# Attention and gated MLP on one core: v's copies loaded by two queues, and the order of all operations read from a table

## Chip, cores and metric

The kernel runs on one core of one Trainium2 chip. The metric is the device time of one execution in microseconds. The core has five engines that work side by side, each through its own list of instructions in a fixed order: TensorE (PE) multiplies matrices, VectorE (DVE), ScalarE (ACT) and GpSimd (POOL) work element by element, and SyncE (SP) starts transfers. Engines wait for each other through semaphores, and a wait at the head of an engine's list holds up all that stands behind it.

## What is computed

Attention with rotary embedding for 8 batches of 8 heads (576 positions, head width 64), and behind it a gated MLP whose gate mixes positions. Cut to what matters:

```python
q_rot, k_rot = (rotate(q), rotate(k))
scores = scale * np.matmul(q_rot, k_rot.transpose(0, 1, 3, 2))
scores = scores - np.max(scores, axis=-1, keepdims=True)
attn = np.exp(scores)
attn = attn / (np.sum(attn, axis=-1, keepdims=True) + 1e-09)
x = np.matmul(attn, v)                      # 8 heads side by side: (8, 576, 512)
...
h = np.maximum(x @ w_in, 0.0)               # 1024 wide
u, v = (h[..., :512], h[..., 512:])
v_n = (v - mu) / np.sqrt(var + 1e-06)       # over the 512 columns
v_s = np.einsum('ts,bsd->btd', w_spatial, v_n) + b_spatial[None, :, None]
return (u * v_s) @ w_out
```

## The kernel before

The work comes in 32 **units** (one batch, two heads) and 8 **MLPs** (one batch each, ready when its four units are done). Units and MLPs overlap: while the units of batch b run, PE fills the gaps between their score tiles with the matmuls of an earlier batch's MLP. The last MLP has nothing left to run beside it.

A unit from number 4 on goes through these steps:

- `prepare` loads q and k (tiles `st`), turns them on POOL, splits them into a rounded part and a rest, and SP copies the halves into the stacked tiles `stk` (ten copies a unit, `stk<-st` and `stk<-lk`), which PE reads.
- `scores` makes nine **score tiles** (128 rows by 576 columns) on PE, L782. A tile lies in one of two PSUM slots (`sc`, two banks each). For each tile DVE takes the maximum (L825), ACT the exponential (L828), which ends the slot's use, and DVE turns the result round in blocks of 32 (L830). PE's next tile but one needs the same slot again.
- `attention` multiplies the nine turned tiles with v, in two halves of 144 matmuls (L741), which use 32 rows of the array each. So v has to lie in the tile `vr` four times, once for each quarter of the partitions. `load_values` loads these four copies (320 KB each) with four transfers on SP. There is one such tile (`vrep`): the load of the next unit waits until the second half of this unit's product is through.
- ACT and DVE copy the product out of PSUM (L758, L759), `normalise` divides by the sums, and the result `x` waits for its MLP.

Units 0 to 3 are done in another way ("plain"): their weights are transposed on PE (L664, L667), copied out by ACT or DVE into one of six places in the tile `turns`, and multiplied there (L710); v is loaded once for them.

An MLP is four groups of matmuls: `pa` (L901, the normalised half), `pb` (L924, the other half), `pc` (L942, the mixing of positions, whose result multiplies u in `gate`) and `pd` (L957, the output). Each step of them is a piece of 2 or 3 matmuls of 288 or 512 columns, into one of four PSUM banks (`pm`), which the products with v use as well.

**What sets the order.** The functions above don't issue instructions. They hand operations to `Program.op`, with an engine, a duration, a due time (`key`, from the constants `K_...`) and the buffers read, written and newly needed. `Program.run` then plays the program through in a model of time: whenever an engine is free it takes, of the operations that are ready, the one with the lowest due time that finds a free slot for its buffers, and issues it. Operations that may run on two engines (`either`, `pair_op`) go to the one that is free first.

## Time and profile before

| | us |
|---|---|
| three runs | 833.79, 834.03, 838.24 |
| median of the runs | 834.03 |
| span of the profiled execution, first to last instruction | 831.4 |
| PE busy in it | 801.3 (96%) |
| PEld (weights loaded for PE) busy | 721.1 (87%) |
| DVE / ACT / POOL busy | 596.6 / 525.3 / 525.5 |

The span leaves out what lies around the first and the last instruction; the median of the runs is 2.6 us above it. PE's end of an instruction is modelled, and consecutive matmuls overlap: a matmul is shown with some 0.3 us, and the next may start 0.13 us after it. So a short stop of PE doesn't show as idle time, and a shown stop is a little longer than what stands there. The granted clock of PE is 0.97 of full speed in the first 50 us and 1.00 after that, the higher of its two levels.

### The profile page before, as it was taken

Reading aid. Unit: us, or ns where it says so; the run is one execution under the profiler, and the core shown is the slowest. Engines: PE = TensorE matmul, PEld = TensorE weight load, DVE = VectorE, ACT = ScalarE, POOL = GpSimd, SP = SyncE. Lnnn points to the kernel's source line nnn. Section 1 sums busy time; section 2 is a strip of 40 time slices with the busy share of each in tenths; the row PEclk is TensorE's granted clock in tenths of the full one; section 3 lists DMA queues with packets and bytes.
Section 4 is the critical chain, followed back from the end, with each engine's and each line's share of the span. In section 5 each row is a group of like instructions: output and inputs, shape, how many; then the busy total and the mean of one; then the engine's idle time right before and its main releaser. Section 6 shows DMA issues by size and latency. Waiting matters only on the chain.

```text
span 831.4 us, 30188 instructions
## 1 busy us (share of the span) xinstructions
PE 801.3 (96%) x12560; PEld 721.1 (87%) x12560; DVE 596.6 (72%) x1179; ACT 525.3 (63%) x1372; POOL 525.5 (63%) x440
## 2 busy tenths in 40 slices
PE   5999988999999999999999999999999999999998
PEld 3565678898899989998889989899899998999898
DVE  6879988886887669867686768776697766875220
ACT  4787877664865568656675648656586565844442
POOL 5998685786675667676566756767486675533221
PEclk9999999999999999999999999999999999999999
DMA  8755574779876777878847786777857778363001
GB/s 326 288 169 166 122 201 122 180 181 222 195 187 167 198 181 181 205 190 226 202 126 193 183 229 171 196 174 193 213 130 205 194 202 207 93 157 86 35 2 58
DMA packets 63867, 144.56 MB, mean 174 GB/s; under 512 B 10993, under 2 KB 12785, under 8 KB 63730
## 3 DMA queue, kind: packets, MB, share of 16 engines
q1 hardware_dynamic: 63730, 142.63, 66.3%
q8 instruction: 99, 1.62, 0.9%
q14 instruction: 38, 0.31, 0.1%
HBM read 93.55 MB, written 9.58 MB: 124 GB/s over the span
## 4 chain that ended last, share of the span: by engine, by line
PE 74%; DVE 7%; ACT 7%; DMA 5%; issue 3%; POOL 2%; SPq 1%; DVEq 0%; ACTq 0%; POOLq 0%
PE psum L741 15%; PE psum L942 14%; PE psum L782 13%; PE psum L957 10%; PE psum L901 9%; PE psum L924 7%; ACT et L828 4%; DMA vr<-in_v_dram 3%; DVE nmx L825 3%; PE psum L802 3%; PE psum L664 2%; PE psum L710 2%; DVE et L830 1%; SPq L416 1%; DVE sm L979 1%
## 5 line engine op out<-in xcount | busy, mean ns | idle before, releaser
L828 ACT ACTIVATE et<-psum,nmx 128x576 f32<-128x576 f32 x288 | 212.7, 740 | 111.1 <-DVE nmx L825 109.3
L825 DVE TENSOR_REDUCE nmx<-psum 128x1 f32<-128x576 f32 x288 | 210.9, 744 | 74.4 <-PE psum L782 64.7
L830 DVE STREAM_TRANSPOSE et<-et 128x576 f32<-128x576 f32 x252 | 192.7, 770 | 42.8 <-ACT et L828 40.7
L541 POOL TENSOR_TENSOR st<-st,tabs 128x576 f32<-128x576 f32 x112 | 163.0, 1468 | 64.1 <-DMA st<-in_qk_dram 49.5
L741 PE MATMUL psum<-et,vr 32*64 32x144 f32 x8064 | 142.7, 285 | 4.1 <-ACT vv L975 1.4
L741 PEld LDWEIGHTS psum<-et,vr 32*64 32x64 f32 x8064 | 126.8, 130 | 17.0 <-issue 11.1
L942 PE MATMUL psum<-wsp,vn 128*128 128x288 f32 x768 | 125.0, 296 | 1.2 <-issue 1.2
L924 PE MATMUL psum<-x,wi 128*128 128x288 f32 x768 | 118.9, 296 | 0.0
L957 PE MATMUL psum<-g,wo 128*128 128x288 f32 x768 | 117.4, 296 | 0.2
L901 PE MATMUL psum<-wi,x 128*128 128x512 f32 x448 | 117.6, 397 | 0.0
L942 PEld LDWEIGHTS psum<-wsp,vn 128*128 128x128 f32 x768 | 109.4, 188 | 2.6 <-issue 2.6
L924 PEld LDWEIGHTS psum<-x,wi 128*128 128x128 f32 x768 | 108.0, 188 | 3.8 <-issue 1.6
L957 PEld LDWEIGHTS psum<-g,wo 128*128 128x128 f32 x768 | 106.5, 188 | 2.5 <-issue 2.4
L782 PE MATMUL psum<-stk 128*128 128x288 f32 x448 | 99.4, 303 | 8.7 <-ACT et L828 8.3
L782 PE MATMUL psum<-stk,stk 128*128 128x288 f32 x448 | 95.7, 295 | 0.1
L901 PEld LDWEIGHTS psum<-wi,x 128*128 128x128 f32 x448 | 79.6, 188 | 16.4 <-issue 2.6
L422 POOL TENSOR_TENSOR g<-u,g 128x288 fp32r<-128x288 f32 x64 | 52.0, 816 | 63.7 <-ACT g L419 63.6
L782 PEld LDWEIGHTS psum<-stk 128*128 128x128 f32 x448 | 72.8, 188 | 19.8 <-ACT et L828 13.2
L545 POOL TENSOR_TENSOR st<-st 128x576 f32<-128x576 f32 x56 | 82.6, 1476 | 2.0
L422 POOL TENSOR_TENSOR vn<-vv,vn 128x512 fp32r<-128x512 f32 x32 | 41.3, 1293 | 61.8 <-ACT vn L419 61.8
L782 PEld LDWEIGHTS psum<-stk,stk 128*128 128x128 f32 x448 | 71.6, 188 | 0.2 <-issue 0.2
L422 POOL TENSOR_TENSOR x<-x,x 128x576 fp32r<-128x576 f32 x64 | 55.6, 890 | 17.2 <-ACT x L419 17.1
(134 smaller groups left out, 1012.3 us busy)
## 6 DMA issues: line engine op xcount, KB each, us to landing
vr<-in_v_dram SPq DMA_DIRECT2D x116, 320.0 KB
st<-in_qk_dram SPq DMA_DIRECT2D x62, 576.0 KB
stk<-lk SPq DMA_DIRECT2D x168, 144.0 KB
stk<-st SPq DMA_DIRECT2D x112, 128.0 KB
out_dram<-ob SPq DMA_DIRECT2D x31, 288.0 KB
ws<-in_w_spT_dram SPq DMA_DIRECT2D x2, 576.0 KB
st<-in_qk_dram SPq DMA_DIRECT2D x2, 288.0 KB
tabs<-in_tab_dram SPq DMA_DIRECT2D x2, 288.0 KB
```

The costliest lines, as they stand in the source:

```text
L422: eng.tensor_tensor(out=lo, in0=src, in1=hi.bitcast(F32), op=ALU.subtract)
L541: f = lambda e: e.tensor_tensor(out=st[j][:, cols], in0=st[j][:, cols], in1=tabs[:, cols], op=ALU.mult)
L545: f = lambda e: e.tensor_tensor(out=st[j][:, :S], in0=st[j][:, :S], in1=st[j][:, S:2 * S], op=ALU.add)
L741: nc.tensor.matmul(bank(g)[64 * h:64 * h + 64, EACH // 9 * (1 - h):EACH // 9 * (1 - h) + EACH], lhsT=vr[rows, b % 4, b // 4, h, :], rhs=e[ ...
L782: nc.tensor.matmul(pt[:, c * 512:c * 512 + HALF], lhsT=lhsT, rhs=rhs[:, c * HALF:(c + 1) * HALF], start=(n == 0), stop=(n == len(parts) - 1))
L825: op(DVE, 680, key + K_MAX, lambda: nc.vector.tensor_reduce(out=nmx.tile, in_=tops(), op=ALU.max, axis=AX.XY, negate=True), r=[pt], w=[nmx ...
L828: op(ACT, 750, key + K_EXP, lambda: nc.scalar.activation(weights(), tops(turn), AF.Exp, bias=nmx.tile, scale=1.0, accum_out=sm[:, to:to + ...
L830: op(DVE, 705, key + K_TURN, lambda: nc.vector.transpose(out=blocks(et, at), in_=blocks(et, at)), w=[(et, at)])
L901: nc.tensor.matmul(pm.tile, lhsT=lhsT, rhs=win[1, d][:, j, :], start=(d == 0 and n == 0), stop=(d == 3 and n == len(todo) - 1))
L924: nc.tensor.matmul(pm[:, :HALF], lhsT=win[0, d][:, i, f * P:(f + 1) * P], rhs=x[d][:, at:at + HALF], start=(d == 0 and n == 0), stop=(d == ...
L942: nc.tensor.matmul(pm[:, :HALF], lhsT=lhsT, rhs=rhs, start=(t == 0 and n == 0), stop=(t == 4 and n == 1))
L957: nc.tensor.matmul(pm[:, :HALF], lhsT=wout[d,][:, i, m * P:(m + 1) * P], rhs=gs[d][:, at:at + HALF], start=(d == 0 and n == 0), stop=(d == ...
```

## The change

In `load_values`, two of the four copies of v (partitions 0 to 63) are still started by SP, the other two (64 to 127) by ACT, with an operation of its own in ACT's list; the product with v then depends on both. `Program.run` no longer decides anything: it issues the operations in the order of a table, `ORDER`, a list of operation numbers; a letter behind a number says on which of its engines an operation that has a choice runs (a: ACT, v: DVE, g: POOL). A second table, `HOME`, gives the slot of each new buffer. The planner's model and most of its constants are gone. A few durations handed to `op` are others and a `mode` is given to it; nothing reads these any more. What each operation computes is as before.

```diff
+ORDER = """
+4 2 60 3 6 8 9 5 10 1 7 11 65 137 138 139 66 67 68 69 71 72 133 74 70 0 76 73 75 81 140v 141 309 77 79 214 12 82 13 78 215 54 22 49 134 84 80 14 83 85
...
+HOME = (
...
     def run(self, make):
-        free = {p: list(range(n)) for p, n in SLOTS.items()}
-        ready = {e: [] for e in LATENCY}
...
+
+        slots = iter(HOME)
+        for word in ORDER.split():
+            o = self.ops[int(word.rstrip("avg"))]
+            assert not o.waits, "an operation comes before one that it waits for"
             for b in o.new:
...
+                b.pool, b.slot = b.pools[0], int(next(slots))
+                b.tile = make(b)
+            o.eng = {"a": ACT, "v": DVE, "g": POOL}.get(word[-1], next(iter(o.costs)))
+            o.f(o.eng)
+            for a in o.after:
+                a.waits -= 1
+        assert next(slots, None) is None
...
-        def fetch():
+        def fetch(start, groups):
             rows = v[b, hp].rearrange("(q j) k h d -> j q (k h d)", q=4)
-            for g in range(4):
-                load(vr[32 * g:32 * g + 32].rearrange("j q k h d -> j q (k h d)"), rows)
-
-        op(DMA, dma_ns(1280, 4, 470, 5.23), key - K_LOAD + 1, fetch, w=[vr], new=[vr])
+            for g in groups:
+                start(out=vr[32 * g:32 * g + 32].rearrange("j q k h d -> j q (k h d)"), in_=rows)
+
+        o = op(DMA, dma_ns(640, 2, 470, 5.23), key - K_LOAD + 1, lambda: fetch(nc.sync.dma_start, (0, 1)), w=[(vr, 0), (vr, 2)], new=[vr])
+        op(ACT, dma_ns(640, 2, 470, 5.23), key - K_LOAD + 1, lambda: fetch(nc.scalar.dma_start, (2, 3)), w=[(vr, 1)], r=[(vr, 2)]).soft = o
...
-        need = [vr, *[(et, n) for n in range(9)]]
+        need = [(vr, 0), (vr, 1), *[(et, n) for n in range(9)]]
```

All five engines' lists change from one end to the other, mostly in small ways: units and MLPs follow each other as before, and neighbours change places. Lines of the file move as well (L782 becomes L786, L828 L831, L901 L904, L957 L960, L416 L420); the two starts of v are L507 now. Three places:

PE, the last score tiles of unit 24 (L782, four matmuls each over two rows: `stk_470` is the stack of the second head, `stk_471` the rests), with output pieces of MLP 4 (L957) between them. Before:

```order
L782 MATMUL psum<-stk_470 128x288 x2
L782 MATMUL psum<-stk_471,stk_470 128x288 x2
L957 MATMUL psum<-g_1_8485,wo_1099 128x288 x3
L782 MATMUL psum<-stk_470 128x288 x2
L782 MATMUL psum<-stk_471,stk_470 128x288 x2
L957 MATMUL psum<-g_2_8642,wo_2277 128x288 x3
L957 MATMUL psum<-g_3_8702,wo_2123 128x288 x3
L782 MATMUL psum<-stk_470 128x288 x2
L782 MATMUL psum<-stk_471,stk_470 128x288 x2
```

The first and the last of these three tiles use the same slot, and 3 + 4 + 6 = 13 matmuls lie between them. Now (the second head's stack is `stk_483`):

```order
L786 MATMUL psum<-stk_483 128x288 x2
L786 MATMUL psum<-stk_484,stk_483 128x288 x2
L960 MATMUL psum<-g_1_8479,wo_1087 128x288 x3
L960 MATMUL psum<-g_3_8729,wo_2120 128x288 x3
L960 MATMUL psum<-g_2_8652,wo_2224 128x288 x6
L786 MATMUL psum<-stk_483 128x288 x2
L786 MATMUL psum<-stk_484,stk_483 128x288 x2
L960 MATMUL psum<-g_3_8729,wo_2120 128x288 x3
L786 MATMUL psum<-stk_483 128x288 x2
L786 MATMUL psum<-stk_484,stk_483 128x288 x2
```

Again the first and the last of the three share a slot; 12 + 4 + 3 = 19 matmuls lie between them.

ACT, unit 16, around the start of its v (L828, then L831: exponentials of the unit's score tiles, named in `nmx` by head and tile; L960, then L963: outputs of MLP 2 out of PSUM). Before:

```order
L828 ACTIVATE et_5558,sums_67<-psum,nmx_0_2_5802 128x18x32
L960 ACTIVATE ob_2_5821<-psum 128x288 x2
L828 ACTIVATE et_5558,sums_67<-psum,nmx_0_3_5831 128x18x32
L828 ACTIVATE et_5558,sums_67<-psum,nmx_1_0_5849 128x18x32
L960 ACTIVATE ob_3_5868<-psum 128x288
L419 ACTIVATE x_5877<-x_15_5770 128x576
L828 ACTIVATE et_5558,sums_67<-psum,nmx_1_1_5880 128x18x32
```

Now:

```order
L831 ACTIVATE et_5548,sums_67<-psum,nmx_0_2_5791 128x18x32
L831 ACTIVATE et_5548,sums_67<-psum,nmx_0_3_5809 128x18x32
L507 DMA vr_5818<-in_v_dram 32x4x640 x2
L831 ACTIVATE et_5548,sums_67<-psum,nmx_1_0_5831 128x18x32
L423 ACTIVATE x_5856<-x_15_5762 128x576
L831 ACTIVATE et_5548,sums_67<-psum,nmx_1_1_5847 128x18x32
```

Two starts of transfers stand between the exponentials of tiles 0_3 and 1_0, and the outputs have moved away from there.

SP, its first transfers: q (`st_0`), k (`st_1`) and the tables of sines and cosines (`tabs`) of unit 0, each in two parts. Before:

```order
L416 DMA st_1_84<-in_qk_dram 128x2x288
L416 DMA tabs<-in_tab_dram 128x2x288
L416 DMA st_0_92<-in_qk_dram 128x2x192
L416 DMA st_1_84<-in_qk_dram 128x2x288
L416 DMA tabs<-in_tab_dram 128x2x288
L416 DMA st_0_92<-in_qk_dram 128x2x384
```

Now:

```order
L420 DMA st_0_79<-in_qk_dram 128x2x192
L420 DMA st_1_81<-in_qk_dram 128x2x288
L420 DMA tabs<-in_tab_dram 128x2x288 x2
L420 DMA st_1_81<-in_qk_dram 128x2x288
L420 DMA st_0_79<-in_qk_dram 128x2x384
```

The first part of q comes first, and the first part of the tables third.

## Rows read from the trace of the kernel before

**Rows 1.** The page's first part: busy time, share of the span and instructions by engine.

```profile
PE 801.3 (96%) x12560; PEld 721.1 (87%) x12560; DVE 596.6 (72%) x1179; ACT 525.3 (63%) x1372; POOL 525.5 (63%) x440
```

**Rows 2.** Busy time by stretch: us, each engine's busy us, clock, DMA share, GB/s.

```profile
0.00:50.00 50.00, 38.75 (x250) 22.96 (x252) 38.21 (x65) 31.57 (x75) 39.51 (x44) 0.97 0.76 276
50.00:100.00 50.00, 47.58 (x361) 30.89 (x357) 44.20 (x73) 43.18 (x112) 42.62 (x33) 1.00 0.54 151
```

**Rows 3.** Who PE waited for: us in total, times, the longest.

```profile
PE psum L782 <- ACT et L828: 8.6, 11, 1.6
PE psum L802 <- DVE st L614: 7.8, 1, 7.8
PE psum L664 <- DVE turns L675: 1.9, 2, 1.7
PE psum L741 <- ACT vv L975: 1.4, 1, 1.4
PE psum L741 <- DVE nmx L825: 1.3, 1, 1.3
```

**Rows 4.** The chain that ended last, a stretch of the last MLP: start, us, what.

```profile
816.54 11.66 PE psum L957 x87
```

**Rows 5.** The page's groups: busy us, mean ns of one, idle before.

```profile
L957 PE MATMUL psum<-g,wo 128*128 128x288 f32 x768 | 117.4, 296 | 0.2
```

**Rows 6.** PE in order of time, unit 24's last tiles: start, us, instruction, [idle before].

```profile
583.58 0.42 PE L782 MATMUL psum<-stk 128*128 128x288 f32 x2
...
584.49 0.42 PE L782 MATMUL psum<-stk 128*128 128x288 f32 x2
...
587.34 0.53 PE L782 MATMUL psum<-stk 128*128 128x288 f32 x2 [1.36 <-ACT et L828]
```

**Rows 7.** PE in order of time, stops at units 4, 16 (two) and 20.

```profile
96.21 0.53 PE L782 MATMUL psum<-stk 128*128 128x288 f32 x2 [1.25 <-ACT et L828]
...
391.29 0.53 PE L782 MATMUL psum<-stk 128*128 128x288 f32 x2 [0.59 <-ACT et L828]
...
392.31 0.40 PE L782 MATMUL psum<-lk,qt 128*128 128x288 f32 x1 [0.23 <-ACT et L828]
...
489.09 0.54 PE L782 MATMUL psum<-stk 128*128 128x288 f32 x2 [0.59 <-ACT et L828]
```

**Rows 8.** Weight loads of the plain units that waited for nothing shown.

```profile
PEld psum L710 <- issue: 5.1, 27, 0.4
```

**Rows 9.** DVE in order of time, the program's start.

```profile
4.97 0.76 DVE L608 TENSOR_TENSOR st<-st,tabs 128x576 f32<-128x576 f32 x1 [4.97 <-DMA tabs<-in_tab_dram]
5.76 0.46 DVE L609 TENSOR_TENSOR st<-st 128x288 f32<-128x288 f32 x1
6.78 0.56 DVE L613 SCALAR_TENSOR_TENSOR st<-st,tabs 128x384 f32<-128x384 f32 x1 [0.56 <-DMA st<-in_qk_dram]
7.37 0.36 DVE L614 TENSOR_TENSOR st<-st 128x192 f32<-128x192 f32 x1
8.38 0.76 DVE L608 TENSOR_TENSOR st<-st,tabs 128x576 f32<-128x576 f32 x1 [0.65 <-DMA tabs<-in_tab_dram]
```

**Rows 10.** The instructions on v's tile: ns of one, least, median, most; and idle causes.

```profile
L416 SPq DMA_DIRECT2D vr<-in_v_dram x116: 317/432/1507, 6.9 to 747.2; - x116
its engine sat idle before it (us, times) until:
  issue: 17.0, 76
  ACT et L828: 3.6, 7
```

**Rows 11.** The chain that ended last, unit 28's v: start, us, what.

```profile
672.94 8.60 DMA vr<-in_v_dram
```

**Rows 12.** PE in order of time, the start of unit 28's product with v.

```profile
688.35 1.92 PE L741 MATMUL psum<-et,vr 32*64 32x144 f32 x105
```

**Rows 13.** The page's group of exponentials on ACT.

```profile
L828 ACT ACTIVATE et<-psum,nmx 128x576 f32<-128x576 f32 x288 | 212.7, 740 | 111.1 <-DVE nmx L825 109.3
```

195 lines of the change are left out of this document (33 added, 162 removed), and 128 rows, old and new, of the table ORDER.

## The prediction

> **What bounds the kernel now.** First the busy times: PE works 801.3 us of a span of 831.4, no other engine over three quarters of it [rows 1]. Then the busy times by stretch: PE is idle 11.2 us of the first 50 and 2.4 of the next 50 [rows 2]; so a third of its idle time lies at the start, and the rest is spread thin. Busy time hides part of a stop: an output matmul is shown with 296 ns [rows 5], but in the last MLP 87 of them take 11.66 us, 0.134 us each [rows 4], so a stop is about 0.16 us longer than the idle time shown. The work itself (matmul counts and sizes) is the same in both kernels. So the change can win only stops of PE, and the view of who PE waited for lists them [rows 3]: 7.8 us until the first tile of unit 0 is there, 11 stops of score tiles (L782) for ACT's exponentials with 8.6 us, the products with v 1.4 + 1.3, the plain units' transposes 1.9. With 11 x 0.16 the score tiles' stops are 10.4 us. Nothing else is large enough to matter.
>
> Why a score tile stops: it needs the slot of the last tile but one, and between the two users PE has only so much other work. In unit 24 the tile of 585 us comes 13 matmuls after the last user, 13 x 0.134 = 1.7 us, and stops 1.36 us; the tile before it came after 16 matmuls (9 output, 4 score, 3 output, by the order), 2.1 us, and its row at 584.49 shows no stop [rows 6]. I call this PE work between two users the **cover**. Counted so over the whole order of before, 8 of 223 pairs have under 1.9 us; the seven pairs with 2.1 stood without a stop. Five of the 11 stops are among the 8: at unit 4 (1.25 shown), at unit 16 (0.59, and 0.23 for the tile behind it), at unit 20 (0.59) and at unit 24 (1.36) [rows 6, 7]; with 0.16 each they make 4.8 us. The other six, 10.4 - 4.8 = 5.6 us, had 2.5 us and more and stopped because DVE or ACT came late.
>
> **The change part by part.**
>
> *Short covers.* In the new order, counted in the same way, 2 of 223 pairs lie under 1.9, both at unit 4; the next is 1.98. Unit 24's place shows it: 19 matmuls, 2.5 us, where 13 were. Unit 4's tiles now follow each other even closer (0.5 us between users), so its 1.4 us stay and grow by some 0.7. Gain 4.8 - 1.4 - 0.7 = 2.7 us; bounds 0 and 4.8.
>
> *Late DVE and ACT.* Whether the six others go depends on how all neighbours fall. The new order may remove all 5.6 us or make half as many new ones; I take half gone, 2.8 us (bounds 5.6 gained and 3 lost).
>
> *Products with v.* The work between a unit's last score tile and its product, counted in the two orders, rises from 2.9 us at least and 4.1 in the middle to 3.5 and 4.8, so the last tile's maximum, exponential and turn are waited for less. Of 1.4 + 1.3 us [rows 3] I take 1.7 as gained; bounds 0 and 2.7.
>
> *Plain units.* Here PE changes between tilings of the array (whole, rows, columns), and after a change the weights come late without a cause shown, 5.1 us in 27 cases, 0.19 each [rows 8]. The orders have 182 and 174 such changes: 8 x 0.19 = 1.5 us. Of the transposes' stops, 1.9 [rows 3], I take half: 1.0. Together 2.5; bounds 0 and 3.4.
>
> *The start.* PE's first matmul waits for k's turn, then q's, on DVE: 0.76 + 0.46 + 0.56 + 0.36 = 2.14 us from the landing of the tables [rows 9]. Before, the tables were second and landed at 4.97; the third transfer landed at 6.78. Now the tables are third, land at about 6.7, and PE starts at 6.7 + 2.14 = 8.8 instead of 7.8. The second part's tables landed at 8.38 and now move up, so some is won back. Cost 0.8; bounds 0 and 1.1.
>
> *v on two queues.* SP drops two of v's four starts in each of 28 units, 2 x 0.432 us [rows 10]. Nothing on PE was late for it: among what PE waited for at v's tile no transfer is named [rows 10], and unit 28's v was there at 672.94 + 8.60 = 681.5, its product began at 688.35 [rows 11, 12]. So landing sooner is worth 0, and the freed SP as well. ACT gains the two starts: 28 x 0.86 = 24 us on an engine with 525 of 831 busy [rows 1]. No trace here shows a start on ACT; SP's own range is 2 x 0.317 to 2 x 1.507 us for the two [rows 10]. Behind them wait the next exponentials and so the score tiles. The starts stand behind work of ACT that already needed the previous product's end, so they add no wait for a semaphore. Two things hide them: ACT is idle 109 us before exponentials anyway, waiting for the maximum, 0.38 per tile [rows 13]; and the covers of the tiles concerned are 2.4 us and more in all units but 4 and 16. With 0.86 on top of the 2.1 us that sufficed, the tiles miss some 4 us in all if nothing else hides them. I take 1.5, nearer to the idle ACT's row; bounds 0 and 24.
>
> *The end.* The last MLP runs alone with PE dense in both; its order within changes nothing: 0.
>
> Sum: -2.7 - 2.8 - 1.7 - 2.5 + 0.8 + 1.5 = -7.4 us. The profiled execution would go from 831.4 to 824.0 us of span; the median of the runs lies 2.6 above the span, 834.0, and becomes **826.6**.
>
> **The rivals.**
>
> *No change.* The stops are only traded. For it: under 3.0 us of cover there are 66 pairs before and 100 now, because the new order evens covers out, and half of the stops' time came at pairs that had 2.5 and more. One late DVE instruction is enough: the new order leaves less above 2.1 than the old one. Then the 8.9 us gained above (the sum without ACT's starts) are paid again at other places: 834 +- 4. Here belongs the case that only the split of v counts: rows 10 to 12 give it no price on PE. The Trainium skill (DMA: Bandwidth & Descriptors, "Issuing engines are not separate DMA queues") says that transfers started by several engines run on the same 16 DMA engines and that this saves no more than the issuing time; by that rule the split alone leaves 834, and the trace, with v there 6.8 us early, agrees. Against the rival: pairs under 1.9 stop by their own count whatever DVE does, and these are nearly gone.
>
> *Slower by ACT.* A start on ACT holds up exponentials for longer than on SP. The place: the two starts of v directly before an exponential, as in unit 16, where the tiles behind have 2.1 us of cover. The price: each unit loses what its starts take over the cover left. It decides the sign at 8.9 / 28 = 0.32 us a unit. With 0.6 us a unit it is 28 x 0.6 = 17 us: 834.0 - 8.9 + 17 = 842. For it: SP's starts reach 1.5 us each [rows 10], and 28 places repeat. The Trainium skill (Perfetto Trace Analysis, "DMA Instruction — HWDGE (DVE, Sync)") says that a start locks the descriptor generator for its own use. By that an ACT start would also wait for one of SP's under way; no run here shows it. Against it: ACT's 109 us of idle time before exponentials, and covers mostly over 2.4.
>
> *Much faster.* All of 10.4 + 2.7 + 3.4 us goes and ACT's starts cost nothing: 834.0 - 16.5 + 0.8 = 818. For it: nothing in PE's work forbids it. Against it: every late DVE instruction would have to vanish too.
>
> **How the numbers follow.** Faster as summed (819 to 829.8): 0.48. Much faster: 0.12. No change: 0.24. Slower by ACT: 0.16, because its price is the only one without a row of its own. A measurement of this kernel can tell about 0.5%, 4.2 us: faster 0.60, same 0.24, slower 0.16. The forecast's own range is 819 to 830. The range for 8 in 10 takes in no change and the cheaper half of the slower case, and at the other end most of the much faster one: 814 to 840.
>
> **What would show it.** In the profile of the changed kernel: PE idle some 7 us less in total, and L786 waiting for ACT's exponentials in about half the time, with unit 4 as the longest stop; the products with v (L746) nearly without waits for DVE and ACT; the first matmul at about 8.8 us; ACT's starts of v (L507) with about 0.43 us each and the exponentials behind them without longer waits of PE; v still landing microseconds before its product. I am wrong if PE's stops at L786 add up to 10 us again at new places (no change), if PE waits for exponentials right behind L507 in most units (slower), or if a start on ACT takes well over 0.6 us.

## The result: 0.6% slower, and the profile after

The median went from 834.4 to 840.8 us, a ratio of 1.0062 with an interval of 1.0044 to 1.0080. The forecast was 826.6, its range ended at 840.0, and the one rival on the slower side (ScalarE's starts hold up the exponentials) isn't what happened. The profiled execution has a span of 841.1 us, where before's had 831.4. First the busy times and the granted clock by slices, from the page of after:

```profile
PE 806.4 (96%) x12560; PEld 727.2 (86%) x12560; DVE 602.0 (72%) x1172; ACT 530.9 (63%) x1379; POOL 528.3 (63%) x440
...
PEclk9999989999999999999999999999999999999999
```

PE has the same 12560 matmuls as in [rows 1], is busy 5.1 us longer and idle 4.6 us longer. One slice of the clock shows an 8, where all of before's slices show a 9:

```profile
PEclk9999999999999999999999999999999999999999
```

Who PE waited for in after (us in total, times, the longest), to be read against [rows 3]:

```profile
PE psum L806 <- DVE st L619: 9.3, 2, 8.2
PE psum L786 <- DMA stk<-lk: 6.9, 4, 3.3
PE psum L786 <- ACT et L831: 5.6, 9, 1.3
PE psum L746 <- issue: 5.0, 5, 1.8
PE psum L669 <- DVE turns L680: 0.9, 2, 0.8
...
PE psum L746 <- DMA vr<-in_v_dram: 0.2, 1, 0.2
```

What was forecast is here: the score tiles wait 5.6 us for exponentials instead of 8.6, the transposes 0.9 instead of 1.9, and the products with v no longer wait for DVE or ACT (2.7 us before). That is 6.7 us gained. Two rows are new. Score tiles stop 6.9 us for **copies** into the stacked tiles, a cause that before doesn't have. And the products with v (L746) stop 5.0 us with no instruction as a cause ("issue"), where before's (L741) stopped 0.8 us:

```profile
PE psum L741 <- issue: 0.8, 2, 0.5
```

With the start (9.3 for 7.8) this is 12.6 us lost. The small rows that I leave out here add up to 2.0 us less in after than in before. The mean granted clock fell from 0.998 to 0.992; 0.006 of 836 us is another 5.0, about the 5.1 us by which PE is busy longer. Together 12.6 - 6.7 - 2.0 + 5.0 = 8.9 us, about the 9.7 by which the spans differ. The profiled execution of after took 842.99 us, 2.2 more than the median. Over many executions the clock's part is smaller too: its mean is 0.9956 in the 18 of after and 0.9977 in 35 of before, 1.8 us of the 5 to 6 that were lost.

A stop hides in busy time too. So I also timed each piece of PE's work from its first matmul to the first of the next piece, and took off the lower quartile of the same kind of piece in before; the sums of this **excess** are:

| us | score tiles | products with v | pa | pb | pc | pd | plain units | all |
|---|---|---|---|---|---|---|---|---|
| before | 13.8 | 4.6 | 4.5 | 7.3 | 4.7 | 8.8 | 11.5 | 55.2 |
| after | 17.7 | 15.0 | 7.5 | 6.3 | 6.0 | 3.7 | 8.1 | 64.2 |

By units, the start of each unit's products says where after falls behind: it is 0.9 us ahead at unit 6 and 0.3 behind at unit 10, then 4.8 behind at unit 11, 5.5 at unit 28 and 9.7 at unit 29. Two places carry it. The longest stop for copies, 3.28 us just ahead of unit 4's product, isn't one of them: after is 3.6 us behind there and 1.6 ahead at unit 5, since before stops in between three times for exponentials (1.08, 0.64 and 1.59 us) and after doesn't.

**The place at 254 to 264 us** (unit 11's first tiles). SP's starts in order of time, then PE's matmuls, then ACT's start of v before them:

```profile
245.71 1.19 SPq L420 DMA_DIRECT2D stk<-st  x1
251.80 3.72 SPq L420 DMA_DIRECT2D rt9d<-rt  x6
255.62 0.50 SPq L420 DMA_DIRECT2D stk<-lk  x1
...
257.61 1.23 SPq L420 DMA_DIRECT2D stk<-lk  x2
```

```profile
257.84 0.56 PE L945 MATMUL psum<-wsp,vn 128*128 128x288 f32 x3
260.16 0.50 PE L786 MATMUL psum<-stk 128*128 128x288 f32 x2 [1.76 <-DMA stk<-lk]
...
260.76 2.88 PE L945 MATMUL psum<-wsp,vn 128*128 128x288 f32 x12
```

```profile
241.63 0.80 ACTq L507 DMA_DIRECT2D vr<-in_v_dram  x2
```

Before unit 11's copies SP starts the six small writes of unit 9's sums (`rt9d`, in `normalise`), 3.72 us, and before these it stands idle for 4.9 us. What it stands there for is, by the trace, a landing of v: the copy that ACT started at 241.63 lands at about 251.8. The small writes don't use v. What ties the two is a semaphore: the program deals out eight of them in turn to the transfers of both queues, and a start waits until the last transfer with its semaphore has landed. The trace has the same one (106) for ACT's copy and for SP's start at 251.80; its last count for the copy comes at 251.78. SP's own waits, after first and then before:

```profile
SPq L420 <- DMA vr<-in_v_dram: 30.7, 25, 4.9
```

```profile
SPq L416 <- DMA vr<-in_v_dram: 42.9, 50, 1.3
```

The waits are fewer but one is 4.9 us long. Then PE stops 1.76 us, and the 12 matmuls behind the stop take 2.88 us; the same 12 take 1.76 at the full clock (in the trace of an experiment below). The clock by stretch (us, busy us of PE, PEld, DVE, ACT, POOL, clock, DMA share, GB/s) shows why:

```profile
258.00:260.00 2.00, 0.40 (x4) 0.17 (x2) 0.46 (x1) 0.44 (x1) 2.00 (x3) 1.00 0.84 197
260.00:262.00 2.00, 1.84 (x10) 1.87 (x11) 0.76 (x1) 0.24 (x1) 0.14 (x1) 0.75 0.85 186
262.00:264.00 2.00, 2.00 (x10) 2.00 (x10) 0.00 (x0) 0.59 (x2) 0.00 (x0) 0.50 0.91 194
```

After a stretch in which PE was busy 0.40 of 2 us, it gets the lower of its two levels, 1.2 GHz, for 3.41 us, which at half speed is up to 1.7 us lost: as much again as in the stop itself.

**The place at 694 to 704 us** (second half of unit 28's product). PE in order of time:

```profile
694.72 1.70 PE L746 MATMUL psum<-et,vr 32*64 32x144 f32 x93
...
698.75 0.71 PE L746 MATMUL psum<-et,vr 32*64 32x144 f32 x22
701.28 3.16 PE L746 MATMUL psum<-et,vr 32*64 32x144 f32 x93 [1.81 <-issue]
```

The product stops in its middle, and 93 of the matmuls behind the stop take 3.16 us at the lower clock, where 93 of the first half take 1.70. The profile names no data that it waits for. Such stops end behind a transfer of the queue that the page calls q8:

```profile
q8 instruction: 99, 1.62, 0.8%
```

99 packets of 16 KB: PE's 2 x 12560 instructions are 98.1 times 256. So PE's own instruction list arrives in pieces of 256. In this trace the packet that belongs here started at 699.0, 14.5 us after the one before it. Where two neighbouring matmuls of a product start more than 0.3 us apart (9 places in after, 3 in before), seven in after and two in before end 1.2 to 1.6 us after the end of such a packet; the profile shows the longer ones as idle time. The products are the part of the program that uses instructions fastest: 144 matmuls and as many weight loads in 2.51 us, 0.017 us a matmul (row below, of e15), where one of the last MLP takes 0.134 [rows 4]. So it is there that PE would run dry first. And other transfers were under way: windows of after (first fence) and of before (second), same columns as above, at unit 28's product:

```profile
694.00:696.00 2.00, 2.00 (x135) 2.00 (x142) 0.00 (x0) 0.00 (x0) 0.00 (x0) 1.00 1.07 304
...
698.00:700.00 2.00, 1.46 (x29) 1.03 (x28) 1.43 (x5) 0.41 (x2) 0.00 (x0) 1.00 0.98 286
```

```profile
689.00:691.00 2.00, 2.00 (x121) 1.80 (x110) 0.00 (x0) 0.00 (x0) 0.00 (x0) 1.00 0.82 201
691.00:693.00 2.00, 2.00 (x46) 1.47 (x51) 0.58 (x1) 0.60 (x1) 0.00 (x0) 1.00 0.01 2
```

In before the DMA engines are nearly empty (0.01) between the two halves of the product. That is no accident of this unit. In before SP starts the six small writes of the unit's sums (3.7 us of SP's time, next to no data) within 2.4 us of the first half of the product in all 28 units, and in 26 of them the next large load only behind them; in after they stand anywhere from 6.4 us before to 19.8 us after. In the 3 us up to the end of an instruction packet for a product, some 10 of the 16 DMA engines are busy on the mean, against some 6 in before.

The weight loads show the same in total, after first:

```profile
PEld psum L746 <- issue: 18.6, 59, 2.1
```

```profile
PEld psum L741 <- issue: 11.1, 47, 0.7
```

### The profile page after: what moved, and what is told of

Its sections match the earlier page's. It is cut to its first block, busy times and chain, and to the rows that moved or that the text cites. A ratio compares the mean times of both kernels' runs of the same rounds, so it can differ in the third digit from the quotient of the medians.

```text
span 841.1 us, 30231 instructions
## 1 busy us (share of the span) xinstructions
PE 806.4 (96%) x12560; PEld 727.2 (86%) x12560; DVE 602.0 (72%) x1172; ACT 530.9 (63%) x1379; POOL 528.3 (63%) x440
## 4 chain that ended last, share of the span: by engine, by line
PE 66%; DMA 10%; DVE 8%; ACT 5%; SPq 5%; issue 4%; POOL 2%; ACTq 0%; DVEq 0%; POOLq 0%
PE psum L746 13%; PE psum L786 13%; PE psum L945 12%; PE psum L960 10%; PE psum L927 8%; PE psum L904 7%; SPq L420 4%; DMA vr<-in_v_dram 4%; DVE nmx L828 2%; DMA stk<-lk 2%; DMA st<-in_qk_dram 2%; ACT et L831 2%; PE psum L806 1%; DMA out_dram<-ob 1%; PE psum L715 1%
## 5 line engine op out<-in xcount | busy, mean ns | idle before, releaser
L831 ACT ACTIVATE et<-psum,nmx 128x576 f32<-128x576 f32 x288 | 212.3, 739 | 116.4 <-DVE nmx L828 112.7
L828 DVE TENSOR_REDUCE nmx<-psum 128x1 f32<-128x576 f32 x288 | 212.4, 746 | 89.7 <-PE psum L786 76.5
L833 DVE STREAM_TRANSPOSE et<-et 128x576 f32<-128x576 f32 x252 | 187.0, 761 | 31.0 <-ACT et L831 30.7
L746 PE MATMUL psum<-et,vr 32*64 32x144 f32 x8064 | 149.0, 290 | 5.4 <-issue 5.0
L746 PEld LDWEIGHTS psum<-et,vr 32*64 32x64 f32 x8064 | 131.3, 133 | 20.1 <-issue 18.6
L927 PE MATMUL psum<-x,wi 128*128 128x288 f32 x768 | 122.5, 297 | 0.7 <-DVE x L763 0.7
L960 PE MATMUL psum<-g,wo 128*128 128x288 f32 x768 | 117.3, 296 | 0.3 <-POOL g L426 0.2
L904 PE MATMUL psum<-wi,x 128*128 128x512 f32 x448 | 117.2, 397 | 0.0
L786 PE MATMUL psum<-stk 128*128 128x288 f32 x448 | 99.6, 304 | 10.9 <-ACT et L831 5.1
L960 PEld LDWEIGHTS psum<-g,wo 128*128 128x128 f32 x768 | 106.6, 188 | 3.0 <-issue 1.6
L786 PE MATMUL psum<-stk,stk 128*128 128x288 f32 x448 | 95.9, 296 | 1.9 <-DMA stk<-lk 1.9
L904 PEld LDWEIGHTS psum<-wi,x 128*128 128x128 f32 x448 | 80.2, 189 | 15.0 <-issue 2.0
L786 PEld LDWEIGHTS psum<-stk 128*128 128x128 f32 x448 | 72.3, 189 | 21.0 <-issue 9.4
L786 PEld LDWEIGHTS psum<-stk,stk 128*128 128x128 f32 x448 | 71.9, 188 | 2.2 <-DMA stk<-lk 1.4
L870 POOL TENSOR_TENSOR x<-x,rb 128x576 f32<-128x576 f32 x32 | 45.7, 1428 | 39.6 <-DVE x L763 18.1
```

The source lines that it names most:

```text
L746: nc.tensor.matmul(bank(g)[64 * h:64 * h + 64, EACH // 9 * (1 - h):EACH // 9 * (1 - h) + EACH], lhsT=vr[rows, b % 4, b // 4, h, :], rhs=e[ ...
L786: nc.tensor.matmul(pt[:, c * 512:c * 512 + HALF], lhsT=lhsT, rhs=rhs[:, c * HALF:(c + 1) * HALF], start=(n == 0), stop=(n == len(parts) - 1))
L828: op(DVE, 680, key + K_MAX, lambda: nc.vector.tensor_reduce(out=nmx.tile, in_=tops(), op=ALU.max, axis=AX.XY, negate=True), r=[pt], w=[nmx ...
L831: op(ACT, 750, key + K_EXP, lambda: nc.scalar.activation(weights(), tops(turn), AF.Exp, bias=nmx.tile, scale=1.0, accum_out=sm[:, to:to + ...
L833: op(DVE, 705, key + K_TURN, lambda: nc.vector.transpose(out=blocks(et, at), in_=blocks(et, at)), w=[(et, at)])
L904: nc.tensor.matmul(pm.tile, lhsT=lhsT, rhs=win[1, d][:, j, :], start=(d == 0 and n == 0), stop=(d == 3 and n == len(todo) - 1))
```

## The experiments

### Which of the two parts: the queue or the order?

`e1_all_on_sp` keeps the table and lets SP start all four copies; `e2_before_two_queues` keeps the planner's order and lets ScalarE start two.

```diff
-lambda: fetch(nc.sync.dma_start, (0, 1))      # e1, on the changed kernel
+lambda: fetch(nc.sync.dma_start, (0, 1, 2, 3))
-lambda: fetch(nc.scalar.dma_start, (2, 3))
+lambda: None
...
-for g in range(4):      # e2, on the kernel before
-    load(vr[32 * g:32 * g + 32].rearrange("j q k h d -> j q (k h d)"), rows)
+start(nc.sync, (0, 1))
+prog.later = [LAG if vr.name == "vr4" else 0, lambda: start(nc.scalar, (2, 3))]
```

> The changed kernel with its table of order as it is, but all four copies of v started by SyncE, in the place where SyncE starts its two now; ScalarE starts none. Theory 'two queues': the new time comes from the second queue. In the changed kernel's trace SyncE stood 4.9 us at 246.9 to 251.8 for a copy of v that ScalarE had started at 241.63, and its next copies of the stacks came that much late. Then this kernel takes 832 to 835 us, SyncE's longest wait for a copy of v falls from 4.9 to under 1.5 us, and PE's stop of 1.8 us at L786 for stk<-lk near 258 is gone. Theory 'order': the time comes from the table. Then it takes 839 to 842 us, and the idle time of the products with v put down to issue stays at about 18 us on the weight loads (11 in the kernel before).

Measured 838.1 us, 1.0044 (1.0016 to 1.0072).

> The kernel before with its planner and its order as they are, and only v's copies for partitions 64 to 127 started by ScalarE, right behind the operation in which SyncE starts the other two (for the first of the 28 units 13 operations behind it). Theory 'two queues': 839 to 842 us, with waits of SyncE for copies of v of 3 us and more, where the kernel before has none over 1.3 us. Theory 'order': 833 to 836 us, as before, and idle time of the products with v put down to issue near 11 us. ScalarE's 56 starts at 0.43 us are 24 us of its time; if they alone were the cost, exponentials behind them would be late and L782's wait for ScalarE would rise over its 8.6 us.

Measured 836.9 us, 1.0023 (0.9998 to 1.0047). So the order alone costs some 0.4%, and the queue alone 0.2%, at the edge of what can be told from nothing. The long wait on SP for a landing of v is 3.0 us in the second and 2.4 in the first, so part of it comes with ScalarE's starts, but the time hardly follows it. Excess inside the products: 16.4 us in the first (15.0 in after), 5.4 in the second (4.6 in before): it follows the order and not the queue. In the first, unit 11's stop for copies shrinks from 1.76 to 0.66 us, and one of 3.30 for an exponential follows 9 us later (its row is below).

### Repairs at single places

`e3_copies_ahead_of_sums` moves one entry of the table, unit 9's small writes, behind unit 11's copies. `e4_load_behind_products` moves the 576 KB load (with what hangs on it) that stands ahead of unit 28's copies behind them and the small writes, and with it behind the product. It also changes PE's list (not shown in the diff): six more matmuls of an MLP, 1.5 us, stand between the two halves.

```diff
 L420 DMA stk_482<-st_0_2949 64x512
-L420 DMA rt9d<-rt_3271 2x4x32 x4
-L420 DMA rt9d<-rt_3271 4x16 x2
 L420 DMA stk_483<-lk_3347 64x576
 L420 DMA stk_483<-st_0_2949 64x512
 L420 DMA stk_482<-lk_3347 64x576
 L420 DMA stk_483<-lk_3347 64x576
 L420 DMA stk_483<-st_0_2949 64x512
 L420 DMA stk_484<-lk_3347 64x576
+L420 DMA rt9d<-rt_3271 2x4x32 x4
+L420 DMA rt9d<-rt_3271 4x16 x2
...
-L420 DMA st_1_10857<-in_qk_dram 128x1152
 L420 DMA stk_482<-lk_10497 64x576
...
 L420 DMA rt28d<-rt_10752 4x16 x2
 L420 DMA stk_484<-lk_10497 64x576
 L420 DMA stk_483<-lk_10497 64x576
+L420 DMA st_1_10994<-in_qk_dram 128x1152
```

> The changed kernel with one operation moved in SyncE's row: the six small writes rt9d<-rt (3.72 us of starts at 251.80) stand behind the six copies stk<-lk and stk<-st of unit 11 and not ahead of them. If these writes are why unit 11's first tile of scores waited 1.8 us for stk<-lk, the stop goes, and with it what came behind it: five matmuls of 0.72 us where 0.40 is usual (the granted clock was at half there, 1.6 us in all) and 0.6 us in the second half of the products with v. Together 4.1 us: 836.5 us. If the copies were late because SyncE was held until 251.8 by ScalarE's copy of v, the first of them starts then instead of at 255.6, and most of the stop goes too. If neither, the time stays at 841 and the stop stands at another copy.

Measured 838.1 us, 1.0032 (1.0006 to 1.0058). The stop for the copies is gone at unit 11, and another of 2.90 us stands right behind it (below, with the run that has both repairs).

> The changed kernel with its order changed at unit 28 alone: the load of 576 KB that SyncE started at 693.57, just ahead of the products with v, starts behind the small writes and copies that follow them, and two matmul groups of the MLP (0.8 and 0.7 us) stand between the two halves of the products. Theory 'instructions late': TensorE stood 3.9 us inside the second half because the packet of queue 8 that brings its instructions went out at 699.0, 14.2 us after the one before, while the 16 engines were full (0.96 to 1.14 from 692 to 700). Then the stall falls under 1 us and the time by 3 to 4 us, to 837. Rival 'chance': such a stall falls on another half of another unit in each execution; then the traces of the other kernels with this table do not show it at unit 28, this one shows it elsewhere, and the time stays at 841.

Measured 839.4 us, 1.0048 (1.0023 to 1.0074). Unit 28's second half then runs its 144 matmuls in 2.51 us without a stop, excess 0.2 us where after has 3.9. Two things were changed at once, the load and PE's list; runs from further down tell them apart. `e5` and `e8` leave PE's list as in after (second half 4.84 us behind the first) and start the load 5 to 6 us later: there too the second half takes 2.51 us. The packet starts 1.9 us behind the begin of the first half in both. In the five traces with the load ahead of the product (after, `e1`, `e3`, `e11`, `e13`) it starts 4.4 to 5.1 us behind it; in the fourteen others, with the load at least 4.1 us behind the begin, 1.7 to 2.7. So the load does hold up the packet there. Of the 3.7 us at the place 0.14%, 1.2 us, came back in the time; with some 0.3% either way on that difference, neither 0 nor all of it can be ruled out.

### Do the repairs add up?

`e15_two_mends` has both repairs, `e16_three_mends` also starts all of v on SP, `e17_four_mends` also has SP's first six transfers in the order of before (tables second).

```diff
-L420 DMA st_0_79<-in_qk_dram 128x2x192      # e17 only
 L420 DMA st_1_81<-in_qk_dram 128x2x288
-L420 DMA tabs<-in_tab_dram 128x2x288 x2
+L420 DMA tabs<-in_tab_dram 128x2x288
+L420 DMA st_0_86<-in_qk_dram 128x2x192
 L420 DMA st_1_81<-in_qk_dram 128x2x288
+L420 DMA tabs<-in_tab_dram 128x2x288
```

> The changed kernel with both single-place repairs at once: the six small writes of unit 9's sums behind unit 11's copies (0.3% won alone, 1.0062 to 1.0032), and the large load of unit 28 behind its products (0.14% won alone, to 1.0048). Places add up: 1.0062 - 0.0030 - 0.0014 = 1.0018 of the kernel before, 836 us. Stops move: what is repaired at one place is paid at another, 1.003 to 1.006, no better than the better of the two alone.

> The same, and all four copies of v started by SyncE again (0.18% won alone, 1.0062 to 1.0044). Places add up: 1.0018 - 0.0018 = 1.0000, 834.5 us: the loss would be accounted for by three causes. Stops move: 1.002 to 1.005.

> The same as the one with three repairs, and SyncE's first six transfers in the order of the kernel before (tables second instead of third; PE waited 9.3 us for the first tiles instead of 7.8). Places add up: another 0.8 to 1.5 us, 0.998 to 0.999, a little faster than before. Stops move: the time at the start comes back by unit 6 or so, since at unit 6 the changed kernel was 0.9 us ahead in spite of its late start: the same as with three repairs, within 0.2%.

Measured 1.0053 (1.0021 to 1.0086), 1.0079 (1.0055 to 1.0103) and 1.0049 (1.0023 to 1.0076): nothing adds up. Two of the three lie clearly above the sum; the interval of the first just misses it. "Stops move" is right, and the run with three repairs lies even above what that allowed. Who PE waited for with two repairs:

```profile
PE psum L786 <- ACT et L831: 9.2, 9, 2.9
...
PE psum L746 <- issue: 1.8, 4, 1.0
...
PE psum L786 <- DMA stk<-lk: 1.4, 2, 1.1
```

The copies' stops went from 6.9 to 1.4 us and the products' from 5.0 to 1.8; the exponentials' went from 5.6 to 9.2 (9.5 and 10.0 in the other two). These sums must be read with care. The longest stop of after, 3.28 us ahead of unit 4's product, is touched by no repair; it is 1.60 here and 3.26 with four, and the profile puts it down to another transfer there (`rt4d<-rt`), so it isn't in the row of copies. And the runs without these repairs differ as well: the exponentials' stops are 5.0 us in `e3`, 7.0 in `e4` and 8.8 in `e1`. What happens can be followed at one place, unit 11, in the trace of two repairs. PE, then ACT, POOL and SP:

```profile
254.41 1.76 PE L945 MATMUL psum<-wsp,vn 128*128 128x288 f32 x12
...
257.29 2.51 PE L746 MATMUL psum<-et,vr 32*64 32x144 f32 x144
262.70 0.83 PE L786 MATMUL psum<-stk 128*128 128x288 f32 x2 [2.89 <-ACT et L831]
```

```profile
260.91 0.68 ACT L423 ACTIVATE x<-x 128x576 fp32r<-128x576 f32 x1 [4.67 <-POOL x L870]
...
261.83 0.72 ACT L831 ACTIVATE et<-psum,nmx 128x576 f32<-128x576 f32 x1
```

```profile
259.48 1.40 POOL L870 TENSOR_TENSOR x<-x,rb 128x576 f32<-128x576 f32 x1 [4.21 <-DMA rb<-rt9d]
```

```profile
250.69 3.71 SPq L420 DMA_DIRECT2D rt9d<-rt  x6
255.29 1.58 SPq L420 DMA_DIRECT2D rb<-rt9d  x2
```

POOL, which waits for unit 9's sums to be back (`rb`), multiplies at 259.48; ACT's next instruction in its list needs that product and stands 4.67 us; the exponential behind it comes at 261.83, and PE stops 2.89 us in front of it. One could put this down to the small writes, which now stand behind the copies. But the same tile, in the traces of `e1`, `e4` and after, where they stand ahead of the copies:

```profile
266.06 0.53 PE L786 MATMUL psum<-stk 128*128 128x288 f32 x2 [3.30 <-ACT et L831]
```

```profile
263.98 0.53 PE L776 MATMUL psum<-stk 128*128 128x288 f32 x2 [1.86 <-ACT et L821]
```

```profile
268.23 0.54 PE L786 MATMUL psum<-stk 128*128 128x288 f32 x2 [0.54 <-ACT et L831]
```

In all of them ACT stands 3.8 to 5.1 us for POOL's product of unit 9's sums. So the late exponential is there in after as well, and PE comes to it late, held up by the copies and the lower clock; where those stops are shorter, it shows. From unit 10's product to unit 11's, after falls 4.5 us further behind before, `e3` and `e15` 4.9 each: at this place the repair of the copies gained nothing, since PE stops 2.9 us for the exponential in both, and the clock falls there as well.

The queue, too, must be read anew. SP alone against two queues is 0.18% shorter with the table (e1 against after), 0.23% shorter with the planner's order (before against e2), 0.26% longer with two repairs (e16 against e15), and 0.36 and 0.63% longer in two pairs below (e6 against e5, e10 against e9). With both signs, the queue's own effect can't be told from zero. The kernels agree on the order: all seven with the table, or with a few entries of it moved, lie 0.32 to 0.79% above before, 0.5% on the mean.

### Is it the place of the small writes?

If the small writes keep the DMA engines clear for the products, putting them there again should win. `e5_sums_at_products` moves them in 28 units so that SP starts them with the first half of the product, as in before (53 entries, with DVE's and ACT's steps ahead of them); `e6_sums_at_products_sp` has v on SP as well. `e7_before_loads_first` is the counter-proof: before's order, but in 22 units the large loads go ahead of the small writes.

```diff
-L461 DMA rt6d<-rt 2x4x32 x4      # e7, on before's order; one of 22 places
-L461 DMA rt6d<-rt 4x16 x2
 L461 DMA st<-in_qk_dram 128x1152
 L461 DMA st<-in_qk_dram 128x1152
+L461 DMA rt6d<-rt 2x4x32 x4
+L461 DMA rt6d<-rt 4x16 x2
```

> The changed kernel with one kind of operation moved in its table, for all 28 units: the six small writes rt<-rt stand in SyncE's row right at the first half of the unit's products with v, as in the kernel before, where they start 2.4 us ahead to 1.9 us behind the half's begin; in the changed kernel it is 6.4 us ahead to 19.8 us behind, and over 3 us behind in eight units. Where the sums they write are made later than that (ten units or so), these few operations of ScalarE and VectorE move with them. Theory 'lull': during their 3.7 us of starts SyncE starts nothing large, the 16 engines run empty, and the packet of instructions that TensorE needs for the second half comes in time; moved away, loads of 576 KB run at that moment and the packet is late. Then the stalls inside the products fall from 15 us (10 to 16 in the four executions with this table) to 6 or less, and the time to 830 to 834. Rival 'copies': the time comes from copies of the stacks that are late, and these small writes only push them back further: stalls inside the products stay over 10 us or stops for stk<-lk grow over 7, and the time stays at 838 or more.

> As the kernel with the small writes at the products, and all four copies of v started by SyncE. If the second queue costs what the pairs so far show (0.2% of the time, 1.0062 against 1.0044 and 1.0023 against 1, each with 0.2 to 0.3 on either side), this one is 1 to 2 us under that one: 828 to 833. If the second queue is free once the products have their lull, the two agree within 1 us.

Measured 906.7 us, 1.0863 (1.0829 to 1.0897), and 910.5, 1.0899 (1.0866 to 1.0932). PE's stops and one wait of SP in the first (L776 are the score tiles there, L410 SP's starts):

```profile
PE psum L776 <- ACT et L821: 18.0, 12, 3.8
PE psum L776 <- DMA stk<-lk: 15.6, 7, 3.9
```

```profile
SPq L410 <- DVE rt L856: 34.9, 14, 12.5
```

SP stands up to 12.5 us for DVE's turn of the sums, and all copies of the next units stand behind it. Nor did the stops inside the products fall: over 2.51 us for each half, the products take 13.0 us more in the first of the two and 13.8 in after. The small writes can't be put back alone: in before all of SP's list is drawn up around them.

> The kernel before, its order written out as a table, with one thing undone: in 22 of the 28 units the one or two loads of 576 KB that follow the six small writes rt<-rt in SyncE's row start ahead of them. All other rows stand as they were. Theory 'lull': the loads now run during the first half of the products with v, the packets of instructions come late, and stalls inside the products rise from 4.6 us to 10 or more, the time by 4 to 8 us, to 839 to 843. Rival 'copies' or 'queue': the small writes start only 0.4 to 0.9 us later, nothing waits for them so soon, and the time stays within 1.5 us of the kernel before.

Measured 834.9 us, 0.9999 (0.9974 to 1.0023). The excess inside the products rose from 4.6 to 8.1 us, and the time didn't. So transfers beside the products do stop them, but 3.5 us of such stops were made good elsewhere. Whether the 10.4 us of after would be too, this run doesn't show. It does show that late small writes alone cost nothing: they start up to 8.0 us behind the begin of their product here, up to 1.9 in before.

### SP's list sorted by need

`e8_row_by_need` sorts SP's 492 operations anew by the time at which their data is ready and needed in after's trace (391 change places); `e9_need_and_products` also changes PE's list at the three products (of units 4, 6 and 28) that stop in all four traces with the table up to then; `e10_need_all_on_sp` has v on SP as well. The table is issued in another order for this, and in these three some steps on shared tiles then take other data, so they don't compute what the kernel before does; number and size of all operations are the same.

```diff
 rt3d<-rt 1x32 x4      # SP's list, unit 4 to 5
 rb<-rt3d 64x576 x2
-stk<-st 64x512
-stk<-lk 64x576
 vr<-in_v_dram 32x4x640 x2
+stk<-lk 64x576 x2
+stk<-st 64x512 x2
+st<-in_qk_dram 128x1152
 stk<-lk 64x576
-stk<-st 64x512
-stk<-st 64x512
-stk<-st 64x512
+stk<-st 64x512 x2
```

> The changed kernel with SyncE's row alone in another order; the rows of the four other engines are word for word those of the changed kernel. At each place the transfer stands next whose data were there in the changed kernel's trace and which is wanted soonest. 391 of 492 operations of the row stand elsewhere, most by a few places. Theory 'late copies': the table lets copies of the stacks wait behind transfers that nobody wants yet. In the kernel before no copy's start ends less than 5.0 us ahead of the first scores that read it, in the changed kernel the shortest are 1.9, 2.0, 2.0, 2.6, 2.8, and the six small writes of unit 9 start 13 us after their data are there. Then stops at L786 for stk<-lk fall from 6.9 us to under 2, and the time by 3 to 6 us, to 834 to 837. Theory 'products': what costs is the supply of instructions in the products with v, and that stays where it is (10 to 16 us in the executions so far), so the time stays at 838 to 841. If both are wrong and the row was right as it stood, it gets slower, as it did when only the small writes were moved (906.7).

> As the kernel with SyncE's row by need, and TensorE's row changed at three places where all four executions with the table show a stall: at unit 4 the first half of the products stands ahead of unit 5's first scores (which waited 1.5 to 3.4 us there), at unit 6 the second half stands 1.7 us earlier (its stall was 1.1 to 2.8 us), at unit 28 two matmul groups more stand between the halves (stall 1.7 to 3.9 us, and 0.2 where they stood so). Together 4.3 to 10 us of stalls, and after each of them the granted clock went to half for 3.4 us, which costs some 1.6 us each. If these places are what the table loses, this kernel takes 5 to 8 us less than the row by need alone and is the fastest of all: 827 to 832. If stalls only move to other places, it stays within 2 us of that kernel.

> As the kernel with both rows changed, and all four copies of v started by SyncE. The two pairs so far put the second queue at 0.2% (1.0062 against 1.0044 with the table, 1.0023 against 1 without, each to 0.2 or 0.3% either way). If it costs that with any order, this one is 1 to 2 us faster than the kernel with two queues; if SyncE's row is now so close that 56 more starts at 0.43 us (24 us in all) hurt it, it is slower by 1 to 3 us.

Measured 1.0397 (1.0369 to 1.0426), 1.0317 (1.0274 to 1.0360) and 1.0380 (1.0344 to 1.0415). In the first, stops for copies fell to 3.5 us, and score tiles waited 14.7 us for exponentials. The three products had no excess left in the second (0.0 to 0.1 us; that of unit 28 had none in the first either). The time fell by 0.8% of the 4% that the sorted list had lost. Sorting SP's starts by what each is needed for, without knowing what they hold up on the other engines, is worse than either order.

### Thirty copies moved, and three products

`e11_tight_copies` starts the 30 copies that came tightest earlier, each where its data is ready; `e12_tight_copies_products` also changes PE's list at the three products as in `e9` and moves unit 28's load as in `e4`.

```diff
-L420 DMA stk<-st 64x512      # one of 30
-L420 DMA stk<-lk 64x576
+L420 DMA stk<-st 64x512 x2
+L420 DMA stk<-lk 64x576 x2
```

> The changed kernel with 30 copies of the stacks, each a start of 0.6 us, moved ahead in SyncE's row by 3 to 12 operations, to where their data were there in the changed kernel's trace, and the six small writes of unit 9 (data there at 238.4, started at 251.80) ahead of unit 10's v. Loads, stores and v's copies keep their order among themselves, and so do all rows of the other engines. Theory 'late copies': these copies are the ones whose landing TensorE or the next load waits for within 1.3 us; ahead, they land 4 us and more before. Then no stop at L786 for stk<-lk is left over 1 us (6.9 us in all in the changed kernel, 3.4 us the longest), and the time falls by 3 to 5 us to 835 to 837. Theory 'products': the stalls inside the products stay at 10 to 16 us and the time at 838 to 841. If stops only move to other rows, the time stays too, and stops at L786 for ScalarE or for other transfers take the place.

> As the kernel with 30 copies moved ahead, and TensorE's row changed at three places: unit 5's first scores behind the first half of unit 4's products, unit 6's second half 1.7 us earlier, and at unit 28 two matmul groups between the halves with the load of 576 KB behind the small writes. In the two kernels with these changes and the whole of SyncE's row by need, the stalls at these three places (3.4, 1.9 and 3.9 us in the changed kernel) were 0.0, 0.0 and 0.1. If the changed kernel's loss is the sum of such places, this kernel takes 8 to 12 us less than it, 829 to 833, and is at or under the kernel before; if not, it stays within 2 us of the kernel with the copies alone.

Measured 846.0 us, 1.0104 (1.0059 to 1.0149), and 844.4, 1.0106 (1.0070 to 1.0143). In the second no row for copies is left among PE's waits. At the head of them stands:

```profile
PE psum L786 <- ACT et L831: 10.6, 9, 4.2
...
PE psum L746 <- issue: 6.0, 6, 1.6
PE psum L746 <- DMA vr<-in_v_dram: 2.5, 4, 0.9
```

All 6.9 us of the copies were won, and 5.0 went to exponentials, 2.3 to v and 1.0 to the products' own stops.

### The products drawn apart, or together

To take the packets out of the question, `e13_halves_apart` puts the second half of each product 2 to 4 pieces later in PE's list, so that PE uses its instructions more slowly. `e14_halves_closer` does the reverse in before: two pieces earlier.

```diff
-MATMUL psum<-et,vr 64x144 x72      # e13, on the changed kernel; one of 28
 MATMUL psum<-stk 128x288 x2
 MATMUL psum<-stk,stk 128x288 x2
 MATMUL psum<-wi,x 128x512 x3
 MATMUL psum<-wi,x 128x512 x3
 MATMUL psum<-wi,x 128x512 x3
+MATMUL psum<-et,vr 64x144 x72
...
+MATMUL psum<-et,vr 64x144 x72      # e14, on the kernel before; one of 28
 MATMUL psum<-x,wi 128x288 x3
 MATMUL psum<-x,wi 128x288 x3
-MATMUL psum<-et,vr 64x144 x72
```

> The changed kernel with TensorE's row changed alone: in each of the 28 units the second half of the products with v stands 2 to 4 matmul groups later (0.4 us each as a rule, 1.2 to 1.6 us in all), so that more of the MLP's and the scores' matmuls lie between the halves. SyncE's row and the starts on ScalarE are as they are. Theory 'products': TensorE's instructions come in packets of 16 KB on queue 8, the halves use a packet up in 2.2 us, and in this table the next one is late because the 16 engines are full when it is due; every stall inside the products ended 1.2 to 1.6 us behind the end of such a packet. With 1.2 to 1.6 us more between the halves the packet has that much longer, most of the 15 us of stalls (10 to 23 in the seven executions with this table) go, and the time falls by 5 to 9 us, to 832 to 836. Theory 'copies' or 'queue': the stalls in the products only take the place of other waits, and the time stays at 838 to 841.

> The reverse on the kernel before, its order written out as a table: in each of the 28 units the second half of the products with v stands two matmul groups earlier (0.8 us), two groups in place of four between the halves as a rule, none in six units. All other rows as they were. Theory 'products': the kernel before has 4.6 us of stalls inside the products because each packet of instructions has just time enough; 0.8 us less gives stalls of 0.4 to 0.8 us in most of 28 units, 10 to 20 us in all, and the time rises by 6 to 15 us, to 841 to 850. If the supply of instructions isn't what decides, the time stays within 2 us of the kernel before.

Measured 902.9 us, 1.0822 (1.0767 to 1.0877), and 879.9, 1.0519 (1.0479 to 1.0560). Halves apart, PE's first waits are:

```profile
PE psum L786 <- ACT et L831: 32.6, 25, 5.5
PE psum L786 <- ACT x L762: 21.7, 24, 2.4
```

Apart from one stop of 0.2 us, no product stops at a packet any more, and "issue" is gone from PE's waits on L746. But the product keeps its slot longer, ACT copies it out later (L762), and the next score tile waits for both. Halves closer in before, PE's weight loads of the products (L786 in that kernel, L741 before):

```profile
PEld psum L786 <- issue: 24.4, 61, 1.9
```

They wait 24.4 us instead of 11.1, and products stop 17 times, for 13.4 us in all, at the end of a packet, where before has two stops with 1.1. So stops at packets can be made by bringing the halves together, and this without fuller DMA engines: by the count used above some 7 of the 16 are busy, hardly more than the 6 of before. The time rose by 45 us, far beyond these 13.4; so this run too shows an effect, and not its price.

## Why the prediction was wrong, point by point

*What bounds the kernel.* Right: PE. That the change can win or lose only PE's stops left out its clock (below).

*Short covers, -2.7 us.* Right: at the counted places in units 16, 20 and 24 no tile waits for its exponential in after, and unit 4's pair grew to 1.34 + 0.50 us, as counted. With 0.16 for each stop, 4.82 us became 2.16: a gain of 2.7.

*Late DVE and ACT, -2.8.* Mis-sized: the other six stops, 5.5 us by the same count, became seven with 4.8, a gain of 0.7. In the runs with two to four repairs all stops for exponentials come to 9.2 to 10.0 us shown, above before's 8.6. So of this term nothing can be counted on; it depends on what else holds up the tiles.

*Products with v, -1.7.* The waits named in [rows 3] went altogether, 2.7 us. But nothing else was looked for there: the stops inside the products, 0.8 us shown in before, became 5.0, and their excess 15.0 for 4.6. The sum has no term for them.

*Plain units, -2.5.* The transposes gained 1.0, as taken. The 1.5 us for changes of tiling didn't come: the weight loads of [rows 8] wait 5.5 us in after, 27 times as before. So the number of changes isn't what these waits follow.

*The start, +0.8.* 1.5: the first matmul at 8.24 instead of 8.8, but another stop of 1.09 behind it. By unit 6 after was ahead again, and e17, which undoes it, is within its interval of the others.

*v on two queues, +1.5.* The sizes of the starts were right and harmless. The starts, on SP and on ACT:

```profile
L507 SPq DMA_DIRECT2D vr<-in_v_dram x56: 317/434/1528, 91.6 to 757.7; - x56
L507 ACTq DMA_DIRECT2D vr<-in_v_dram x56: 317/410/1502, 91.7 to 762.3; - x56
```

0.41 us on ACT, 0.43 on SP, and PE's waits for exponentials fell; so the rival "Slower by ACT" is refuted with its condition (0.32 us a unit on PE's path). Its sentence on the Trainium skill (Perfetto Trace Analysis, "DMA Instruction — HWDGE (DVE, Sync)"), a start that waits for the other engine's, has no row here: both ranges are the same. PE waited 0.2 us for v, so "landing 0" held on PE. It failed on SP, which wasn't looked at: its longest wait for a landing of v went from 1.3 to 4.9 us, with the next units' copies behind it. What the split of v costs in all can't be told from zero (`e2`: 1.0023, 0.9998 to 1.0047).

*The terms that are missing.* This is the step that failed. The prediction adds up the kinds of stops that before shows, and its list of them ends with "Nothing else is large enough to matter". SP has no term of its own but "the freed SP", worth 0 since "nothing on PE was late for it"; that SP's starts follow each other in a new order, with the copies among them, isn't weighed at all. That nothing was late in before says that its order left room, not that there is room: by my count from the traces, the shortest times from a copy's start to the first tile that reads it were 5.0 to 6.3 us in before and are 1.9 to 2.8 in after. What came in place of 0 are 6.9 us of stops for copies. The second omission is PE's instruction list as a transfer like the others. The page of before has its queue, and "issue" stood in its waits with 11.1 us of weight loads. The Trainium skill (Runtime: NRT & Kernel Launch, "Instruction fetch mechanics") tells of blocks of 256 instructions and of a cost at each that is mostly hidden; the trace agrees on the blocks, and shows that with products that use a block in little over 2 us it isn't hidden: up to 2 us a time. That is 4.2 us more of stops than in before. The third is the clock: three times it fell to half for 3.4 or 6.8 us at stops of 1.8 us and more, once in before (besides its last microsecond), and the prediction priced a stop at its length and 0.16 us.

*The rivals.* "No change: the stops are only traded" had the mechanism: 6.7 us gained and 12.6 lost. The sign that it gave came true, stops at L786 of 10 us and more (13.2: 6.9 for copies, 5.6 for exponentials, 0.7 for DVE). But it put the trade within the exponentials, so it ended at 834 and not at 841. That this could come out above 0 by other stops was the case that was missing, and with it the range.

What stays open: how much of the 0.5% is the copies', how much the packets' and how much the clock's. Each can be taken away at its place, and at each attempt (e3, e4, e11, e12, e15) others grew; no run takes away one of them in the whole program and leaves the rest as it is. None of the versions beats the kernel before.

## What to carry to other kernels

An order that is close to balanced can't be improved by counting one kind of stop: list, for each queue that the new order touches, the least time between when a thing is started and when it is needed, before and after, since what was never late has no row in the waits. Whether that number could have been had from the new order alone, before it ran, isn't shown here. A stop that is taken away is worth its length only if the next wait in line, on the same piece of work, ended earlier; read that from the trace before adding gains up. And a forecast made of many small gains of one engine should carry a case in which another engine's list loses as many.

## What the runs showed of the hardware

- PE's instructions come in packets of 256 on a DMA queue of their own (q8, 99 packets of 16 KB). Where PE runs through them fast, it stops in the middle of a product and goes on 1.2 to 1.6 us after a packet's end (seven times in after, 6.0 us; 17 times, 13.4 us, in `e14`). A large load started just ahead delays the packet: at unit 28 it starts 4.4 to 5.1 us behind the product's begin with the load ahead (five traces), 1.7 to 2.7 with the load at least 4.1 us behind (fourteen).
- The two issuing queues weren't independent in this program, since their transfers share eight semaphores in turn: SP stood 4.9 us before a start of its own until a copy of v had landed that ACT had started. With one queue the longest such wait is 1.3 us in before and 2.4 in `e1`.
- At stops of PE of 1.8 to 3.3 us in after, the granted clock fell to 0.50 for 3.4 us and more, and the same 12 matmuls took 2.88 us for 1.76. The runs' mean clock is 0.998 in before's and 0.994 to 0.996 with the table; it is 0.996 in `e2` too, which keeps before's order.
